# Shifting one weight-conversion step by four slots, starting the last conversion later, and new engine tables, in an attention + SwiGLU kernel

## The chip, the core and the metric

The kernel runs on one core of a Trainium2 chip. The metric is device time in microseconds (us), lower is better. Five engines work side by side, each through its own queue in program order: TensorE (PE: matmuls, and PEld for its weight loads), VectorE (DVE), ScalarE (ACT), GpSimd (POOL) and SyncE (SP), which here only issues DMAs. Semaphores tie them together: an instruction waits until those that it depends on are done, and everything behind it on its own queue waits too.

## What is computed

All arrays are float32.

```
q, k, v: (8 batches, 8 heads, 576 tokens, 64);  tau = 0.02
scores = q k^T / 8
scores = where(scores >= rowmax(scores) - tau, scores, -1e9)
attn   = exp(scores - rowmax) / (sum + 1e-9)
x      = (attn v), heads side by side                # 4608 x 512
g      = x @ w_gate;  val = x @ w_val                # 512 -> 1536
out    = (g * sigmoid(g) * val) @ w_out              # 1536 -> 512
```

Weights arrive as 64-bit floats. The kernel turns each one into a 32-bit float itself, from the two 32-bit words of every number.

## The kernel before

**Two phases.** The first batch is treated apart from the other seven. It runs as 20 *first-batch slots*, one for each tile of 128 queries (64 in a last tile) of a pair of heads. Segments `n` = 0 to 3 hold two tiles each, segments 4 to 7 three; `x` counts tiles in a segment. The fifth slot is (n, x) = (2, 0), the ninth (4, 0), the tenth (4, 1). The other batches run as *main slots* s = 0, 1, 2, ..., twelve to a batch, three to a pair of heads.

**A first-batch slot** (function body after `last = iter(())`): PE computes scores (`sc`, L438, or L444 for a 64-row tile) into one of two PSUM buffers per tile half; DVE takes the negated row maxima (`nm`, L455); ACT computes thresholds and exponentials (L458, L459); DVE masks them and sums them (L462), then L464 and L465 give the reciprocal `ri`; from the ninth slot on one half of the tile is scaled by ACT (L472) and the other by POOL (L470). In the next slot PE transposes the tile (`tp`, L506; L508 in the first eight slots) and ACT copies it out (L515, L519, L522); in the slot after, PE multiplies with v (`xa`, L539, L541). From the ninth slot, PE fills in matmuls of the gate and value products (`pg`, `pv`, L555).

**Weight steps.** There are 24 pieces of 128 x 768 elements, numbered here from 0 in the order of their fetches: 16 of w_gate and w_val, 8 of w_out. Each takes:

1. *fetch* (`fetch_weights`, L282 as a pair of DMAs or L279 as one, on SP). It is issued only when the landing place is free;
2. *split* (`split_weights`, ACT, L298 and L299), the sign-free high part and the low part;
3. *clamp* (POOL, L291; `clamp_split`);
4. *shift* (`shift_weights`, DVE, L318);
5. *join* (`join_weights`, DVE, L324), in the next slot just after L455; it frees the landing place;
6. *add* (`add_lower`, POOL, L334): one directly after the joins of the slot, one more behind the scaling L470 and the clamp L291 of the same slot, if pieces wait.

In steady state slot k splits piece k-2, shifts piece k-3 and joins piece k-4. A last tile of a segment in segments 4 to 6 is a *double* slot: it shifts two pieces behind its matmuls, and the slot after joins two. `shift_weights` and `fetch_weights` in a slot move whatever is next in line, so that holding one step back moves all later pieces back by a slot until a slot takes two.

Between these come other steps: SP issues the loads of q, k and v (L367, L417, L418), 8 at a time in flight by its semaphores; POOL scales the queries (L371, with the whole `qT` of segment 8 in the tenth slot); DVE transposes them (L669, L754).

**The main slots** are written by a planner (class `Plan`). Each instruction is a job with an engine, an estimated duration, dependencies and a rank; whenever an engine is free in the plan, the ready job of the best rank and earliest time is emitted next. So the order of each queue follows from estimated times, and a small edit reorders much. In a main slot DVE takes maxima (`mx`, L1726, L1728); a copy across partitions is done by DVE (L1734, L1735) or, for slots in `FIRST_MAX_BY_ACT`, by ACT (L1740, then L1744 on DVE); then come thresholds (L1747), six exponentials (L1751), six masks (L1753), an exchange of sums (L1761), `ri` (L1766, L1767), six scalings by ACT (L1779) or, for as many as `FIRST_POOLED` says, by POOL (L1776), and three transposes (L1781). The scores of slot s+1 (L1705) need the masks of slot s, because they reuse its PSUM.

The two tables hold for main slots 0 to 23 (batches 1 and 2). `rest_of_weights` plans what is left of the weights at main slot 0: the last pieces 21 to 23, with ACT jobs L873 and L876, a clamp on DVE (L291) for the last two, L883 and L885 on DVE (shift and join) and L887 on POOL (add). Only piece 23 is still to be fetched then (L864). Weight pieces that were fetched earlier count as landed at plan time 6.3; the one still to be fetched is ready for L873 when its planned DMA ends.

Of the kernel before, what the change touches and what calls it, by code (L numbers as in the profile page):

```python
# [27 lines left out]
class Plan:  # L28
# [12 lines left out]
    def job(self, eng, took, fn, *deps, rank=1, lag=0.0, moves=0.0):  # L41
        j = Job(eng, took, fn, rank, lag, moves)
        for d in deps:
            if isinstance(d, Job) and d.end is None:
                d.then.append(j)
                j.waits += 1
            elif d is not None:
                j.ready = max(j.ready, self.after(d, eng) if isinstance(d, Job) else d + self.HOP)
        if not j.waits:
            self.open[eng].append(j)  # L50
        return j
# [61 lines left out]
def kernel(  # L113
# [14 lines left out]
    NP = H // 2  # L128
# [106 lines left out]
    def give_back(ps):  # L235
        turns.append(taken.pop(id(ps))[0])

    def run_idle(n):
        ps = bank("idle")
        for _ in range(n):  # L240
            nc.tensor.matmul(ps[:, 0:TC], ones[:, 0:P], ones, start=True, stop=True)
        give_back(ps)
# [62 lines left out]
    def clamp_split():  # L305
        while unclamped:
            dst = unclamped.popleft()
            clamp(nc.gpsimd, dst)
            clamped.append(dst)

    def shift_weights(n=1):

        steps = [split.popleft() for _ in range(min(n, len(split)))]
        if any(up is x for up, place, lo in steps for x in unclamped):
            clamp_split()
        for up, place, lo in steps:
            ub = up.bitcast(U32)
            nc.vector.tensor_scalar(out=ub, in0=ub, scalar1=3, scalar2=None, op0=ALU.logical_shift_left)  # L318
        shifted.extend(steps)

    def join_weights():
        for up, place, lo in shifted:
            ub = up.bitcast(U32)
            nc.vector.scalar_tensor_tensor(out=ub, in0=words(place, up, 1), scalar=0x80000000, in1=ub,  # L324
                                           op0=ALU.bitwise_and, op1=ALU.bitwise_xor)
            used.discard(place)
        unsummed.extend(shifted)
        shifted.clear()
        add_lower(min(1, len(unsummed)))
# [348 lines left out]
    def give(unit):  # L678
        ready.append(unit)
        left[0] += cost(unit)  # L680
# [19 lines left out]
    for n, seg in enumerate(segs[:2 * NP]):  # L700
        early_slots[0] = n < NP
        if n >= NP:
            seg["v"] = segs[seg["i"]]["v"]
        for x, t in enumerate(seg["tiles"]):
            go = scores(seg, t)
            next(go)
            join_weights()
            if not n and not x:
                run_idle(6)
            next(last, None)  # L710
            box = []
            if n < NP:
                attend_tile(lambda *y: box.extend(y))
            else:
                attend_tile()
            flips = flip_steps()
            if n >= NP and x == 1:
                next(flips, None)
            next(go)
            if box:  # L720
                box[1]()
                give_back(box[0])
            next(last, None)
            for _ in flips:
                pass
            if n == NP and x == 0:
                attend_tile()
                give(FIRST)
            part = pace(n, x) / 2
            more = len(split)  # L730
            if n or x:
                split_weights()
                fetch_weights(2)
            next(go)
            clamp_split()
            add_lower(1)
            double = t == NT and NP <= n < NP + 3
            if more and not double:
                shift_weights()
            fill(part)  # L740
            next(go)
            fill(part)
            if double:
                shift_weights(2)
                split_weights()
                clamp_split()
                fetch_weights(2)
            gates()
            last = go
            if n == NP - 1 and x == 0:  # L750
                later.rotate(1)
            if later and (n == NP or n == NP - 1 and x == 0):
                to, fr = later.popleft()
                nc.vector.transpose(out=to, in_=fr)  # L754
            if x == 0 and 0 < n < NP - 1:
                load_v(segs[n + 1])
                more_loads.popleft()()
            if n == 0 and x == 1 or n == 1:
                scales.popleft()()
            elif n == NP - 2 and x == 1:  # L760
                more_loads.popleft()()
                scales.popleft()()
            elif n == NP - 1:
                scales.popleft()()
                fetch_qk(NP)
            elif n == NP and x == 1:
                scales.popleft()()
            if x == len(seg["tiles"]) - 2 and n + 1 < len(segs):
                prepare(segs[n + 1])
# [8 lines left out]
    job, pe = plan.job, plan.pe  # L778
# [72 lines left out]
    def rest_of_weights():  # L851

        todo = [(dst, None, place, lo) for dst, place, lo in split] + [(dst, None, place, None) for dst, place in fetched]
        landed = 6.3
        todo += [(dst, srcs, place, None) for dst, srcs, place in wpieces]
        done, joins = {}, []
        for n, (dst, srcs, place, lo) in enumerate(todo):
            m = dst.shape[1]
            j = None
            under = done.get((NW // 3 - len(todo) + n) // 2)  # L860
            if srcs:
                def fetch(dst=dst, srcs=srcs, place=place):
                    to = places[place].bitcast(U64).rearrange("p (m n) -> p m n", m=nf)
                    nc.sync.dma_start(out=to, in_=srcs[0])  # L864

                j = job("SP", 0.1, fetch, done.get(place), lag=5.0)
            if lo is None:
                lo = los[0].rearrange("p (m n) -> p m n", m=m)
                los.rotate(1)
                before = joins[-3] if len(joins) > 2 else None  # L870

                def up_part(dst=dst, place=place):
                    nc.scalar.activation(dst, words(place, dst, 1).bitcast(F32), AF.Abs, scale=2.0 ** -96)  # L873

                def lo_part(dst=dst, place=place, lo=lo):
                    nc.scalar.activation(lo, words(place, dst, 0), AF.Identity, bias=minus2, scale=-2.0 ** -51)  # L876

                j = job("ACT", 0.93, up_part, j if srcs else landed, done.get(place), under, rank=2)
                j = job("ACT", 1.03, lo_part, j, before, rank=2)
            ub = dst.bitcast(U32)  # L880
            if not any(dst is x for x in clamped):
                j = job("DVE", 0.6, lambda dst=dst: clamp(nc.vector, dst), j, rank=2)
            j = job("DVE", 0.6, lambda ub=ub: nc.vector.tensor_scalar(  # L883
                out=ub, in0=ub, scalar1=3, scalar2=None, op0=ALU.logical_shift_left), j, rank=2)
            j = job("DVE", 0.96, lambda ub=ub, dst=dst, place=place: nc.vector.scalar_tensor_tensor(  # L885
                out=ub, in0=words(place, dst, 1), scalar=0x80000000, in1=ub, op0=ALU.bitwise_and, op1=ALU.bitwise_xor), j, rank=2)
            j = job("POOL", 1.85, lambda ub=ub, lo=lo: nc.gpsimd.tensor_tensor(out=ub, in0=ub, in1=lo.bitcast(U32), op=ALU.add), j, rank=2)  # L887
            joins.append(j)
            done[place] = j
        return joins  # L890
# [1013 lines left out]
    CH = {0: 2, 1: 3, 10: 4, 11: 4}  # L1904
    POOLED = {1: 3, 3: 2, 6: 3, 7: 2, 11: 1}
    MAX_BY_ACT = (0, 3, 5, 6, 8, 9, 10)
    FIRST_POOLED = {0: 2, 1: 2, 4: 1, 6: 1, 7: 2, 8: 2, 10: 1, 11: 1, 12: 2, 13: 2, 14: 3, 15: 3, 17: 2, 18: 1, 19: 3, 20: 1, 21: 1, 22: 1, 23: 3}
    FIRST_MAX_BY_ACT = (0, 1, 2, 3, 6, 9, 12, 15, 16, 18, 20, 21)
    CD = {0: 1, 1: 1, 9: 2, 10: 2, 11: 2}
    PLAIN = {0: 2, 1: 2, 2: 3, 3: 1, 4: 2, 5: 3, 6: 1, 7: 2}  # L1910
    CH0 = {8: 3, 9: 2, 10: 4, 11: 3, 12: 2}
# [42 lines left out]
    for s, (n, x) in enumerate((n, x) for n in range(len(halved)) for x in range(NU3)):  # L1954
# [13 lines left out]
        elif s == 1:  # L1968
            box = []
            m = pe(1.0, lambda: attend_tile(lambda *y: box.extend(y)))  # L1970
            j = job("ACT", 0.27, box[1], m, rank=0)
# [4 lines left out]
        if s == 1:  # L1976
            prepare_v(seg)
        at_, pooled, max_by_act = (kk, POOLED, MAX_BY_ACT) if b > DEEP else (s, FIRST_POOLED, FIRST_MAX_BY_ACT)
        slot_rest(seg, t, pss, mark, pooled.get(at_, 0), at_ in max_by_act, 1 if x == NU3 - 1 else 2)
        if x == 0 and n + 1 < len(halved):  # L1980
            prepare_next(i + 1, plan.t)
        if s == 0:
            joins = rest_of_weights()
# [3 lines left out]
        if s in WS:  # L1987
            g, place = WS[s]
# [24 lines left out]
    for c in (B - 1, B):  # L2013
# [4 lines left out]
        if c < B:  # L2018
            w = SM // 2
            j = []  # L2020
# [43 lines left out]
```

## Time and profile before

| what | value |
|---|---|
| median of 3 runs | 1373.76 us (1372.51 to 1375.14) |
| profiled execution | 1371.38 us, of which the program's span is 1369.2 us |
| PE busy in the span | 1351.0 us, 99% |
| DVE, ACT, POOL busy | 78%, 64%, 53% |
| PE idle from 0 to 160 us of the span, summed over 10 us stretches | 11.4 us |
| PE idle from 160 to 420 us | 1.4 us |
| granted TensorE clock, all 10 us stretches to 420 us | 1.00 |
| first-batch slots end, main slot 0 begins (first L1705) | 130.69 us |

The profile is of one execution, and all steps are worked out against its own times; what lies around its span is 1371.38 - 1369.2 = 2.2 us. Its views are: a page of totals; the chain of waits that ended last (at each step what released it); the list of who waited for whom; and a timeline of instructions with their start, duration, engine, line and, in brackets, the idle time of the engine before it and what ended it. Matmul ends are modelled, so an idle PE is counted only where the next matmul starts late.

### The profile page before, as it was taken

To read this page: it belongs to the slowest core of one execution; us is meant where nothing else is said; L and a number is where in the kernel's file an instruction comes from. 1 tells how busy PE (TensorE), PEld (TensorE's weight loads), DVE (VectorE), ACT (ScalarE), POOL (GpSimd) and SP (SyncE) were. 2 spreads that over 40 slices of the span, in tenths; PEclk is the share of its full clock that TensorE was granted. 3 is DMA by queue.
4 is the path that set the end of the run, shared out by engine and by line. 5 is a ranking of instruction groups with operands and counts; after the bars stand their busy time and mean duration, and the time that the engine had idled before them with its cause. 6 is when DMAs were issued, how large, how long until landed. Compare 5 with 4: busy or idle time off the path is not lost.

```text
span 1369.2 us, 39187 instructions
## 1 busy us (share of the span) xinstructions
PE 1351.0 (99%) x15590; PEld 1116.1 (82%) x15590; DVE 1070.9 (78%) x2815; ACT 875.5 (64%) x2277; POOL 719.9 (53%) x665
## 2 busy tenths in 40 slices
PE   8999999999999999999999999999999999999998
PEld 7777787778788788877887888877887788999998
DVE  7878888887887777777778777777777776787786
ACT  6888776666756766677776766776767764330330
POOL 2688598663564669434973387427943593000000
PEclk9999999999999999999999999999999999999999
DMA  8752424545525540654154513553165403524411
GB/s 177 200 185 90 82 60 133 146 121 156 151 52 155 144 98 27 181 159 117 37 171 128 150 36 128 144 144 87 36 192 144 113 19 143 162 78 146 151 66 32
DMA packets 208294, 162.32 MB, mean 119 GB/s; under 512 B 166128, under 2 KB 180464, under 8 KB 202736
## 3 DMA queue, kind: packets, MB, share of 16 engines
q1 hardware_dynamic: 203920, 158.86, 41.3%
q8 instruction: 124, 2.03, 0.6%
q10 hardware_dynamic: 4192, 0.95, 0.3%
q14 instruction: 58, 0.48, 0.1%
HBM read 138.28 MB, written 21.50 MB: 117 GB/s over the span
## 4 chain that ended last, share of the span: by engine, by line
PE 90%; DVE 3%; DMA 2%; POOL 2%; SPq 1%; issue 1%; ACT 1%; ACTq 0%; DVEq 0%; POOLq 0%
PE pb L993 18%; PE pa L993 12%; PE px L1473 12%; PE sc L1705 10%; PE pe L993 9%; PE xa L1802 9%; PE po L1269 5%; PE py L1482 5%; PE sc L1154 2%; PE pg L1200 2%; PE pv L1200 2%; PE pe L1154 1%; SPq L367 1%; DMA wo<-in_moe_w_val_dram 1%; PE sc L1473 1%
## 5 line engine op out<-in xcount | busy, mean ns | idle before, releaser
L1753 DVE SCALAR_TENSOR_TENSOR pall<-sc,th,pall 128x288 f32<-128x288 f32 x504 | 244.0, 514 | 65.1 <-ACT pall L1751 50.7
L993 PE MATMUL pb<-xall,big 128*128 128x256 f32 x1152 | 273.5, 380 | 0.0
L1751 ACT ACTIVATE pall<-sc,nm 128x288 f32<-128x288 f32 x504 | 232.2, 498 | 34.1 <-DVE pall L1753 33.8
L993 PEld LDWEIGHTS pb<-xall,big 128*128 128x128 f32 x1152 | 216.4, 190 | 31.0 <-issue 2.2
L1781 DVE STREAM_TRANSPOSE pall<-pall 128x576 f32<-128x576 f32 x252 | 189.7, 765 | 58.2 <-ACT pall L1779 41.4
L1779 ACT ACTIVATE pall<-pall,ri 128x288 f32<-128x288 f32 x415 | 189.8, 529 | 26.3 <-DVE ri L1767 25.8
L846 POOL TENSOR_TENSOR hall<-hall,tmp 128x512 f32<-128x512 f32 x80 | 102.3, 1279 | 159.3 <-DVE hall L1046 141.9
L993 PE MATMUL pa<-xall,big 128*128 128x256 f32 x768 | 183.4, 382 | 0.0
L993 PEld LDWEIGHTS pa<-xall,big 128*128 128x128 f32 x768 | 143.0, 190 | 22.2 <-issue 2.7
L1705 PE MATMUL sc<-kT,qT 64*32 64x144 f32 (+1 forms) x5376 | 150.0, 345 | 2.9 <-DVE pall L1753 1.7
L1726 DVE TENSOR_REDUCE mx<-sc 128x2 f32<-128x576 f32 x168 | 124.8, 743 | 28.6 <-PE sc L1705 28.1
L1705 PEld LDWEIGHTS sc<-kT,qT 64*32 64x32 f32 x5376 | 97.8, 106 | 56.9 <-issue 21.0
L993 PE MATMUL pe<-xall,big 128*128 128x256 f32 x576 | 137.2, 381 | 0.4 <-issue 0.4
L1802 PE MATMUL xa<-pall,vall 64*32 64x288 f32 x4032 | 133.0, 404 | 0.9 <-DVE hall L1046 0.8
L1776 POOL TENSOR_SCALAR pall<-pall,ri 128x288 f32<-128x288 f32 x89 | 88.9, 1010 | 67.0 <-DVE ri L1767 63.8
L993 PEld LDWEIGHTS pe<-xall,big 128*128 128x128 f32 x576 | 108.5, 190 | 17.3 <-issue 2.8
L1802 PEld LDWEIGHTS xa<-pall,vall 64*32 64x32 f32 x4032 | 76.5, 107 | 50.6 <-issue 7.4
L1761 ACT COPY sums<-sums 32x6 f32<-32x6 f32 x336 | 66.8, 199 | 45.6 <-DVE pall L1753 41.1
L1045 ACT ACTIVATE vall<-tmp 128x512 f32<-128x512 f32 x96 | 60.2, 630 | 24.6 <-DVE tmp L1058 9.0
L1482 PE MATMUL py<-wo,hall 128*128 128x256 f32 x336 | 74.8, 379 | 0.0
L1728 DVE TENSOR_REDUCE mx<-sc 128x1 f32<-128x288 f32 x168 | 74.8, 445 | 0.0
L846 POOL TENSOR_TENSOR tmp<-tmp 128x512 f32<-128x512 f32 x36 | 45.9, 1276 | 53.4 <-ACT tmp L1068 53.4
(258 smaller groups left out, 2481.3 us busy)
## 6 DMA issues: line engine op xcount, KB each, us to landing
big<-sums_hbm SPq DMA_DIRECT2D x42, 1024.0 KB, 5.4
big<-sums_hbm SPq DMA_DIRECT2D x48, 768.0 KB, 4.7
vall<-in_v_dram SPq DMA_DIRECT2D x112, 144.0 KB, 3.0
out_dram<-big SPq DMA_DIRECT2D x32, 256.0 KB, 3.0
qT<-in_q_dram SPq DMA_DIRECT2D x112, 72.0 KB, 4.8
kT<-in_k_dram SPq DMA_DIRECT2D x112, 72.0 KB, 3.0
wo<-in_moe_w_gate_dram SPq DMA_DIRECT2D x16, 384.0 KB, 4.1
wo<-in_moe_w_val_dram SPq DMA_DIRECT2D x16, 384.0 KB, 4.8
```

Of the source, the lines that this page charges most:

```text
L846: return lambda: nc.gpsimd.tensor_tensor(out=out, in0=a, in1=b, op=op)
L993: nc.tensor.matmul(ps[:, i], w[:, k_, i * P:(i + 1) * P], x[:, k_, :], start=first and i == k_ == 0, stop=True, skip_group_check=True)
L1473: nc.tensor.matmul(ps, a[:, f, :], ws[n][:, f, :], start=bank_ not in begun, stop=True, skip_group_check=True)
L1482: nc.tensor.matmul(ps(), a[:, f, i * P:(i + 1) * P], operands[o][:, f, :], start=first and f == 0, stop=True, skip_group_check=True)
L1705: nc.tensor.matmul(pss[h][(slice(g * G, (g + 1) * G), *part)], qT[hs, col:col + G], kT[hs, c * SH + keys[0]:c * SH + keys[1]], start=True, ...
L1726: rs.append(job("DVE", 0.72, lambda n=n, tile_=tile_: nc.vector.tensor_reduce(out=mx[:, n:n + 2, 0], in_=tile_[:, :, 0:SH], axis=AX.X, op= ...
L1751: ej = job("ACT", 0.42, lambda x=x, n=n: nc.scalar.activation(ps[x], scs[x], AF.Exp, bias=nm[:, n:n + 1]), ej, *((masks[h, 0], masks[h, 1] ...
L1753: masks[x] = job("DVE", 0.45, lambda x=x, n=n: nc.vector.scalar_tensor_tensor(out=ps[x], in0=scs[x], scalar=th[:, n:n + 1], in1=ps[x], op0 ...
L1776: scaled.append(job("POOL", 1.02, lambda x=x, n=n: nc.gpsimd.tensor_scalar(out=x, in0=x, scalar1=ri[:, n:n + 1], scalar2=None, op0=ALU.mul ...
L1779: scaled.append(job("ACT", 0.46, lambda x=x, n=n: nc.scalar.activation(x, x, AF.Copy, scale=ri[:, n:n + 1]), rj, rank=rank))
L1781: seg["turned"].append(job("DVE", 0.72, lambda both=both: nc.vector.transpose(out=both, in_=both), *scaled, rank=rank))
L1802: nc.tensor.matmul(holds[a].ap()[x * G:(x + 1) * G, 0:SH].rearrange("d (i q) -> d i q", q=G), vr[rs, h, j, ds], p[rs, h, :, j, :], start=( ...
```

## The change

Three edits:

- **The step in the fifth slot is left out** (`(n, x) != (NP - 2, 0)`, with NP = 4), and **the ninth slot shifts two pieces** (`1 + (n == NP and x == 0)`). Pieces 2 to 5 are thus shifted and joined one slot later each; in the ninth slot pieces 5 and 6 are shifted, in the tenth both are joined; from piece 7 on everything is in its old slot.
- **A weight that is still to be fetched at main slot 0 (piece 23) is not ready for L873 before plan time 19.0**; it had been ready when its DMA was planned to end.
- **Both tables have new entries.** The number of scalings on POOL changes in main slots 3, 6, 8, 12 to 17 and 21 to 23; ACT takes over the exchange of maxima in slots 10, 17 and 23, and gives up that of slot 16.

```
-            if more and not double:
-                shift_weights()
+            if more and not double and (n, x) != (NP - 2, 0):
+                shift_weights(1 + (n == NP and x == 0))
...
-        landed = 6.3
+        landed, begins = 6.3, 19.0
...
-                j = job("ACT", 0.93, up_part, j if srcs else landed, done.get(place), under, rank=2)
+                j = job("ACT", 0.93, up_part, *((j, begins) if srcs else (landed,)), done.get(place), under, rank=2)
...
-    FIRST_POOLED = {0: 2, 1: 2, 4: 1, 6: 1, 7: 2, 8: 2, 10: 1, 11: 1, 12: 2, 13: 2, 14: 3, 15: 3, 17: 2, 18: 1, 19: 3, 20: 1, 21: 1, 22: 1, 23: 3}
-    FIRST_MAX_BY_ACT = (0, 1, 2, 3, 6, 9, 12, 15, 16, 18, 20, 21)
+    FIRST_POOLED = {0: 2, 1: 2, 3: 1, 4: 1, 6: 3, 7: 2, 8: 1, 10: 1, 11: 1, 12: 3, 13: 1, 15: 2, 16: 3, 17: 3, 18: 1, 19: 3, 20: 1, 22: 2, 23: 2}
+    FIRST_MAX_BY_ACT = (0, 1, 2, 3, 6, 9, 10, 12, 15, 17, 18, 20, 21, 23)
```

How the queues stand after the change, by the programs alone (no times): PE's order is the same. On SP the fetch of piece 6 goes from ahead of the second group of four query loads (`extra<-in_q_dram`, L367) to behind it, and that of piece 7 from ahead of the eight loads of `qT` and `kT` to behind them. On DVE one L318 and one L324 go from the fifth and sixth slot to the ninth (two L318) and the tenth (two L324 between L455 and L462). On POOL the tenth slot's order becomes L334, L470, L291, L334, L371, where it had been L334, L470, L291, L371. ACT's order is the same until main slot 1; there L873 of piece 23 goes from ahead of L1740 to behind the exponentials and L1209, ahead of L1761. On DVE, L885 of piece 23 goes to main slot 3, between the maxima and L1744. From main slot 4 on, the jobs of DVE, ACT and POOL are reordered in places down to slot 23.

## The prediction

> **What bounds the kernel now.** I read the page's totals first, then who waited for whom on PE, then the chain of waits around the slots that the diff touches, then the timeline of single instructions.
>
> ```profile
> PE 1351.0 (99%) x15590; PEld 1116.1 (82%) x15590; DVE 1070.9 (78%) x2815; ACT 875.5 (64%) x2277; POOL 719.9 (53%) x665
> ```
>
> PE is busy 99% of 1369.2 us, and the diff leaves its instructions and their order alone. The time can move only by the places where PE stands still: it can win no more than the waits now there, and it loses whatever new wait it causes. PE's waits from 57 to 157 us (total, how often, longest):
>
> ```profile
> PE sc L438 <- DVE pall L462: 2.2, 3, 0.9
> PE tp L506 <- POOL pall L470: 1.4, 3, 0.5
> PE sc L1705 <- DVE pall L1753: 1.2, 1, 1.2
> PE pg L1200 <- ACT big L522: 0.6, 1, 0.6
> ```
>
> So in the first batch PE's scores wait for DVE's masks. The chain of waits says why (start, duration, what; parts of it from 57 to 92 us):
>
> ```profile
> 62.80 0.87 DVE big L324
> 63.66 1.58 DVE pall L462 x4
> ...
> 67.64 1.05 POOL big L291
> 68.69 1.70 POOL qT L371
> 70.39 1.80 POOL big L334
> 72.19 1.11 POOL big L291
> 73.33 0.04 DVE big L318
> ...
> 75.62 1.94 DVE big L324 x2
> 77.56 1.49 DVE pall L462 x4
> ```
>
> From the tenth slot on, the end is set by DVE's join and masks, then by POOL without a gap, then by DVE again, up to the scores at 78.44. Work added to this row of steps is added to the time.
>
> **Edit 1, what is taken out of the fifth and sixth slots.** Away go one shift (L318 at 33.07, 0.88 us) and one join (L324 at 36.20, 1.46 us) ahead of the masks at 37.58, for which PE waited:
>
> ```profile
> 38.54 1.94 PE L438 MATMUL sc<-pall,qT 64*128 64x288 f32 x8 [1.09 <-DVE pall L462]
> 40.05 0.91 ACT L298 ACTIVATE big<-wo 128x768 f32<-128x768 f32 x1 [1.37 <-DMA wo<-in_moe_w_val_dram]
> 42.21 1.05 PE L508 MATMUL tp<-pall 128*128 128x128 f32 x7 [0.28 <-ACT pall L478]
> ```
>
> The 1.09 us at the scores would go. But PE's next step but one, the transposes at 42.21, already waits 0.28 us for ACT's L478, and that stands in ACT's queue behind the split L298, which waited 1.37 us for a weight DMA (issued 34.24, landed 39.97). The edit brings that DMA no earlier, so ACT still ends L478 at about 42.2 and PE starts the transposes at 42.21. The wait at the scores becomes a wait at the transposes: **gain 0** (at most the 1.09, if that DMA came earlier too).
>
> **Edit 1, SP's queue.** Joins that come a slot later free landing places later. Piece 6's pair of DMAs, issued at 43.19 and 43.59, goes behind four query loads, to about 45.0; by the trace's median of 4.9 to 5.5 us for such a pair it lands near 50, and its split ran at 50.42: about 0.3 us to spare. Piece 7's pair, issued at 46.12 and 46.55, goes behind eight loads of qT and kT, which were issued from 47.49 to 54.93. It is then issued between some 51 and 55.6, landing between 56 and 59.95 (the pair issued at 55.04 and 55.64 landed then). Its split stands at 57.78 in ACT's queue, ahead of L472, which releases PE's transposes at 61.40 with 1.1 us to spare. I take 0, the value of the earlier issue; the later one delays L472 by 2.2 us and PE by 1.1. Range 0 to +1.2.
>
> **Edit 1, the step given back.** The ninth slot's second shift lies in DVE's idle 4.19 us ahead of L455 at 61.38: 0. In the tenth slot a second join comes between L455 and the masks:
>
> ```profile
> 62.72 0.95 DVE L324 SCALAR_TENSOR_TENSOR big<-wo,big 128x768 uint32<-128x768 uint32 x1
> 65.79 1.88 POOL L470 TENSOR_SCALAR pall<-pall,ri 128x576 f32<-128x576 f32 x1 [0.22 <-DVE ri L465]
> 70.36 1.83 POOL L334 TENSOR_TENSOR big<-big 128x768 uint32<-128x768 uint32 x1
> 78.44 1.82 PE L438 MATMUL sc<-pall 64*128 64x288 f32 x9 [0.82 <-DVE pall L462]
> ```
>
> One more join is 0.95 us; the masks, `ri` at 65.45 and POOL's L470 at 65.79 come that much later. Behind the new wait on POOL stand L291, L371, L334 and L291, back to back to 73.29, and DVE's shift waits for the last. Among them comes one more add, L334 of piece 6, between L291 and L371: 1.83 us. (The other L334, ahead of L470, was there already and ends at 65.57, in time.) Both terms lie on the chain that ends at 78.44: 0.95 + 1.82 = **+2.77**; PE's wait there becomes some 2.7 to 3.6 us. From below: +1.8, if the join were hidden but the add not. From above: 1.46 for the join (its cost at 36.20) and 2.46 for the add (the longest at 76.76), +3.9. I take 2.77, since most neighbours of the same shape take 0.95 and 1.82. I expect no recovery behind it: the next waits of this kind fall at 98.10 and 117.78, a period of 19.66 us, a loop of PE, DVE and POOL in which each waits for the other, and the slots after are unchanged.
>
> A sentence of the Trainium skill speaks against such a wait. The row first: the granted clock is 1.00 in every 10 us stretch to 420 us, with no PE wait over 1.17 us there after the start. The page "TensorE: Matmul & The Clock Gate", section "Why this matters for your kernels", allows no PE gap over about 3 us, and its Part 1 gives half clock after an idle window of about 3.4 us. The new wait of 2.7 to 3.6 us comes close to it; no run here shows one, and by the page a closed gate would add an estimated 1.7 us (half of a 3.4 us window), by the row nothing. The sum leaves it out.
>
> **Edit 2, the last split begins later.** In main slot 1 ACT held up the exchange of maxima for a weight DMA, issued 140.08 and landed 146.52:
>
> ```profile
> 146.54 0.93 ACT L873 ACTIVATE wo<-extra 128x768 f32<-128x768 f32 x1 [0.41 <-DMA extra<-in_moe_w_out_dram]
> 147.49 0.81 ACT L1740 COPY mx<-mx 32x6 f32<-32x6 f32 x4
> 153.06 1.32 PE L1705 MATMUL sc<-kT,qT 64*32 64x288 f32 x19 [1.17 <-DVE pall L1753]
> ```
>
> With L873 gone from there, L1740 starts near 146.6, 0.9 earlier, and the exponentials lose L876 ahead of them too: from 149.43 to about 147.95. The masks, which ended at 153.34, end about 1.4 earlier, near 151.95, and PE, free at 151.89, starts without the 1.17 us. These scores also ran stretched by the masks (one per 1.84 us where others take 1.43): 0.41 more. Less 0.2 for a new small wait: 1.17 + 0.41 - 0.2 = **-1.35** (0 to -1.58). What is late next: the join L885 of piece 23 moves to main slot 3, between the maxima and L1744 (at 171.23). It costs 0.94 to 1.38 us by the other joins, and that slot's masks (end 175.31) have only 0.19 us ahead of the next scores (175.50): 1.1 - 0.2 = **+0.9** (0.3, if half of it lies in the 0.20 and 0.16 us idle that DVE has there, to 1.2).
>
> **Edit 3, the tables.** From main slot 3 to 23, PE's remaining waits at the scores are 0.41 (at 184.78), 0.41 (215.94), 1.2 (279.5), 0.5 (291.3) and 0.64 (344.35): 3.2 us. In slot 4 the transpose L1846 (0.78 at 183.44) goes from between the masks to ahead of them, which I value at -0.35 of the 0.41; in slot 13 a scaling less on POOL gives -0.3, in slot 14 one more on DVE's side +0.25; the other changed slots have 1.3 to 3.5 us between masks and next scores, which cover a transfer of one scaling (0.53 on ACT). I take **-0.35**; ends -3.2 (all waits gone) and +1.0 (new ones in slots 12 to 17).
>
> **Sum.** 2.77 - 1.35 + 0.9 - 0.35 = +1.97. Against the profiled execution's own 1371.38 (span 1369.2 and 2.2 around it) that is 1373.35. The median of the three runs is 1373.76, 2.4 above the profiled one, so the predicted median is 1373.76 + 1.97 = **1375.7**.
>
> **Rivals.**
> - *Slower, plainly:* piece 7's weights land late on ACT's queue in the ninth slot. For it: eight loads now go ahead of them on SP. Against it: each load is small, and 46 to 55 us has pauses. It decides once they land after about 58.9 (57.78 + 1.1). Price +1.1, beside the add at its contended 2.46 (+0.6): 1375.7 + 1.1 to 1.7, about **1377.2**.
> - *Faster:* ACT's splits and POOL's clamps don't depend on PE and run on while PE waits at 78.44; then the later waits, 0.7 each at 98.10 and 117.78 and three of 0.5 at the transposes, up to 2.8 us, vanish and pay edit 1 back. For it: POOL waited 1.54 us for ACT's L298 at 93.63. Against it: the loop runs through PE. With the forecast's other terms -0.8; with all of the tables' 3.2 us and 0.3 for L885, -4.25. That is 1369.5 to 1373.0, its middle **1371.2**.
> - *The change does nothing that shows:* the add finds room after all, edits 2 and 3 return what 1 takes, within 0.5 of **1373.8**.
>
> **How the numbers follow.** 0.2%, or 2.75 us, is about what a measurement of this kernel can tell from no change. Forecast 0.42, its own range 1374.2 to 1377.3, with 0.27 within 0.2% and 0.15 slower; the late weights 0.25, all slower; the payback 0.25, with 0.15 faster and 0.10 within; no effect 0.08. Faster 0.15, same 0.45, slower 0.40. The range must reach into both other cases: 1371.0 leaves out 0.13 of the payback case, 1378.6 leaves out 0.07 of the others.
>
> **What would show it.** Right: scores of the 12th slot near 81 instead of 78.44 with PE waiting 2.5 us or more; two L324 back to back at 62.7 and POOL without a gap from L470 to the last L291; transposes at 42.2 still waiting, now about 1.4 us; no wait at main slot 1's end, a new one of 0.9 at the scores near 175.5. Wrong: main slot 0 beginning no later than 130.69, L298 near 57.8 waiting for a DMA, waits at 98 and 118 gone, or a granted clock under 1.00.

## The result, and the profile after

Twenty executions of each kernel: the changed one has a median of 1374.72 us (1373.31 to 1377.09), the one before 1372.74 (1369.92 to 1375.14). The ratio is 1.0017, 95% interval 1.0011 to 1.0024. By the medians that is 1.98 us longer, with 1375.7 and +1.97 predicted. The profiled execution took 1374.33 us, its span 1372.5 against 1369.2.

The forecast's sum came out. Not all of its terms did, as the profile after shows. The page's totals:

```profile
PE 1353.8 (99%) x15590; PEld 1116.7 (81%) x15590; DVE 1068.8 (78%) x2807; ACT 875.1 (64%) x2284; POOL 719.8 (52%) x666
```

The same 15590 matmuls keep PE busy 2.8 us longer than before. So a part of the loss is no wait at all: the matmuls ran slower. Who waited for whom on PE from 57 to 157 us (total, times, longest):

```profile
PE sc L438 <- DVE pall L462: 4.8, 3, 3.2
PE tp L506 <- POOL pall L470: 0.9, 2, 0.5
PE pg L1200 <- ACT big L522: 0.6, 1, 0.6
PE sc L444 <- DVE pall L462: 0.6, 1, 0.6
```

The wait of 1.2 us at the main slots' scores (L1705) is gone; one wait of 3.2 us at the first batch's scores is new. The chain of waits up to it:

```profile
63.15 1.73 DVE big L324 x2
...
68.77 1.05 POOL big L291
69.82 1.78 POOL big L334
71.60 1.70 POOL qT L371
73.30 2.09 POOL big L334
75.39 0.81 POOL big L291
76.23 0.04 DVE big L318
...
79.13 1.73 DVE big L324 x2
80.86 0.75 DVE pall L462 x2
```

This is the forecast's chain with the second join at its head (63.15) and the second add in its middle (69.82). PE's timeline at the two places that edit 1 touches:

```profile
37.46 1.72 PE L438 MATMUL sc<-pall,qT 64*128 64x288 f32 x8
42.62 2.05 PE L508 MATMUL tp<-pall 128*128 128x128 f32 x16 [2.00 <-ACT pall L478]
65.67 1.19 PE L444 MATMUL sc<-pall 64*64 64x288 f32 x8 [0.56 <-DVE pall L462]
81.74 3.21 PE L438 MATMUL sc<-pall 64*128 64x288 f32 x10 [3.23 <-DVE pall L462]
```

The wait at the seventh slot's scores is gone (37.46, no bracket) and stands at the transposes instead, 2.00 us. The scores at 81.74 come 3.30 us later than before, and they took 3.21 us where the same ten took 2.06. The view by stretches shows why; the columns are the stretch, busy time of PE, PEld, DVE, ACT and POOL, then the granted clock, the DMA share and GB/s:

```profile
78.00:80.00 2.00, 0.51 (x3) 0.11 (x1) 2.00 (x4) 1.50 (x4) 0.52 (x1) 1.00 0.00 0
80.00:82.00 2.00, 0.26 (x1) 0.29 (x2) 2.00 (x4) 1.63 (x4) 1.93 (x1) 0.97 0.46 65
82.00:84.00 2.00, 2.00 (x9) 1.78 (x9) 1.20 (x6) 1.44 (x2) 1.63 (x2) 0.50 1.03 402
84.00:86.00 2.00, 2.00 (x19) 1.12 (x18) 1.68 (x3) 0.23 (x1) 2.00 (x3) 0.50 0.81 324
86.00:88.00 2.00, 2.00 (x10) 2.00 (x11) 2.00 (x1) 0.65 (x2) 1.34 (x1) 0.50 0.00 0
88.00:90.00 2.00, 2.00 (x10) 1.80 (x9) 1.15 (x4) 2.00 (x6) 1.77 (x1) 0.82 0.43 57
```

PE stands still from 78.5 to 81.7, and the granted clock then falls to 0.50 for 6.8 us. Below this is called half clock, or the clock gate closing. How far the changed kernel lies behind the one before, by the start of PE's scores, is the ledger of the whole change:

| scores that start in the changed kernel at | behind by | what happened since the line above |
|---|---|---|
| 60.46 (tenth slot) | 0.36 | transposes at 42.62 |
| 72.22 (twelfth) | 0.89 | second join |
| 81.74 (thirteenth) | 3.30 | second add on POOL, a slower shift, shorter joins |
| 90.77 (fourteenth) | 6.21 | half clock |
| 136.16 (main slot 0) | 5.47 | a later wait at the transposes that vanished |
| 157.29 (main slot 2) | 4.23 | edit 2 |
| 179.50 (main slot 4) | 4.00 | edit 2, with L885 |
| 406.20 (main slot 24) | 3.50 | edit 3 |

### The profile page after: what moved, and what is told of

The parts are those of the page before. It is cut to its first block, busy times and chain, and to the rows that moved or that the text cites. A ratio compares the mean times of both kernels' runs of the same rounds, so it can differ in the third digit from the quotient of the medians.

```text
span 1372.5 us, 39182 instructions
## 1 busy us (share of the span) xinstructions
PE 1353.8 (99%) x15590; PEld 1116.7 (81%) x15590; DVE 1068.8 (78%) x2807; ACT 875.1 (64%) x2284; POOL 719.8 (52%) x666
## 4 chain that ended last, share of the span: by engine, by line
PE 92%; DVE 2%; POOL 2%; DMA 1%; SPq 1%; issue 1%; ACT 0%; ACTq 0%; DVEq 0%; POOLq 0%
PE pb L993 18%; PE pa L993 12%; PE px L1473 12%; PE sc L1705 10%; PE pe L993 9%; PE xa L1802 9%; PE po L1269 5%; PE py L1482 5%; PE pg L1200 2%; PE pv L1200 2%; PE sc L1154 2%; PE pe L1154 1%; SPq L367 1%; PE sc L1473 1%; PE sc L438 1%
## 5 line engine op out<-in xcount | busy, mean ns | idle before, releaser
L1705 PE MATMUL sc<-kT,qT 64*32 64x144 f32 (+1 forms) x5376 | 149.3, 345 | 1.7 <-issue 1.0
L1705 PEld LDWEIGHTS sc<-kT,qT 64*32 64x32 f32 x5376 | 97.4, 106 | 55.9 <-issue 19.1
L1761 ACT COPY sums<-sums 32x6 f32<-32x6 f32 x336 | 66.5, 198 | 45.4 <-DVE pall L1753 40.8
L1740 ACT COPY mx<-mx 32x6 f32<-32x6 f32 x196 | 38.1, 194 | 59.6 <-DVE mx L1728 57.7
```

The lines of the kernel that those rows point to most:

```text
L1705: nc.tensor.matmul(pss[h][(slice(g * G, (g + 1) * G), *part)], qT[hs, col:col + G], kT[hs, c * SH + keys[0]:c * SH + keys[1]], start=True, ...
```

## The experiments

Each kernel ran with the kernel before on the same chip, the ratios being to that. What the executions' mean granted clock says turned out to be the key, so the table has it. One window of half clock is 3.41 us (shown below) and lowers the mean by about 0.001; an execution at 1.000 is called open.

| kernel | median us | before, same chip | ratio, 95% interval | executions at clock 1.000 / 0.999 / less | median at 1.000 |
|---|---|---|---|---|---|
| edit 1 alone | 1375.80 | 1370.89 | 1.0034 (1.0020 to 1.0048) | 0 / 0 / 6 | - |
| edit 2 alone | 1369.67 | 1370.89 | 0.9994 (0.9983 to 1.0005) | 6 / 2 / 4 | 1368.74 |
| edits 2 and 3 | 1369.28 | 1370.89 | 0.9988 (0.9978 to 0.9999) | 5 / 2 / 5 | 1368.24 |
| changed, PE kept busy in its wait | 1372.74 | 1370.89 | 1.0008 (0.9997 to 1.0018) | 5 / 4 / 2 | 1370.99 |
| before, 6 memsets | 1376.45 | 1371.37 | 1.0035 (1.0024 to 1.0047) | 0 / 0 / 12 | - |
| before, 14 memsets | 1378.87 | 1371.37 | 1.0053 (1.0038 to 1.0067) | 0 / 0 / 6 | - |
| changed, one add later | 1374.30 | 1371.37 | 1.0016 (1.0008 to 1.0024) | 0 / 3 / 9 | - |
| before, PE kept busy at the seventh slot | 1370.66 | 1371.37 | 0.9992 (0.9983 to 1.0002) | 7 / 4 / 1 | 1370.65 |
| edits 2 and 3, PE kept busy there | 1370.03 | 1372.91 | 0.9978 (0.9969 to 0.9987) | 8 / 0 / 2 | 1369.90 |
| the same, one transpose earlier | 1369.60 | 1372.91 | 0.9978 (0.9968 to 0.9988) | 7 / 0 / 1 | 1369.52 |
| before, 3 memsets | 1376.81 | 1372.91 | 1.0020 (1.0010 to 1.0031) | 0 / 3 / 9 | - |
| edit 3 alone | 1374.73 | 1372.91 | 1.0009 (0.9998 to 1.0021) | 3 / 0 / 8 | 1371.62 |
| the kernel before, with rows 1 to 4 | 1370.89 | | | 12 / 5 / 13 | 1369.83 |
| the kernel before, with rows 5 to 8 | 1371.37 | | | 11 / 6 / 12 | 1370.50 |
| the kernel before, with rows 9 to 12 | 1372.91 | | | 10 / 3 / 18 | 1370.92 |

All 20 executions of the changed kernel had a mean clock of 0.996 to 0.998. Of the 90 of the kernel before in the last three rows, 33 had 1.000. Where a kernel's executions fall into groups by the clock, its median moves with their shares, so that the difference of two medians and the ratio can be about 1 us apart (the changed kernel with one add later, and 3 memsets).

**1. Edit 1 alone.**

```
+            if more and not double and (n, x) != (NP - 2, 0):
+                shift_weights(1 + (n == NP and x == 0))
```

> The kernel before with edit 1 alone. Theory A (the wait closes the clock gate): PE waits about 3.2 us for the masks near 78.5, the granted clock falls to 0.50 for some 6 to 7 us behind it, and main slot 0 begins about 5.5 us later than the kernel before (136.2 instead of 130.7); the time is 4.5 to 5.5 us longer. Theory B (the forecast's +2.77 is right and the half clock of the changed kernel was a chance of one execution or comes from edits 2 and 3): granted clock 1.00, time 2.5 to 3 us longer.

It took 4.9 us more than the kernel before, PE waited 3.2 us at the thirteenth slot's scores, the clock was low in all six executions, and main slot 0 began at 135.70. Theory A: edit 1 carries the loss, and the half clock belongs to it.

**2. Edit 2 alone.**

```
+        landed, begins = 6.3, 19.0
+                j = job("ACT", 0.93, up_part, *((j, begins) if srcs else (landed,)), done.get(place), under, rank=2)
```

> The kernel before with edit 2 alone (the old tables). Theory A: the wait of 1.17 us at the end of main slot 1 goes and L885 finds room, so the scores of main slot 4 come 1.2 to 1.4 us earlier and the time is 1 to 1.5 us shorter. Theory B (the forecast): L885 gives 0.9 us back at main slot 3, and the time is 0.45 us shorter.

The median is 1.2 us shorter, that of the executions at clock 1.000 1.1 us (1368.74 against 1369.83); the interval reaches past 1. In the traces, the way from main slot 0's scores to main slot 23's is 258.30 us against 259.80. So -1.1 to -1.5, theory A. The profiled execution brought something that nobody had asked for. Its scores of the seventh slot, and the clock behind them (columns as above):

```profile
39.37 2.65 PE L438 MATMUL sc<-pall,qT 64*128 64x288 f32 x8 [1.98 <-DVE pall L462]
```

```profile
38.00:40.00 2.00, 0.63 (x3) 0.55 (x4) 1.97 (x6) 1.52 (x5) 1.43 (x1) 1.00 1.00 359
40.00:42.00 2.00, 2.00 (x9) 1.04 (x7) 1.44 (x4) 1.67 (x2) 1.04 (x2) 0.62 1.04 363
42.00:44.00 2.00, 2.00 (x18) 1.67 (x17) 1.94 (x3) 2.00 (x7) 1.45 (x3) 0.50 0.97 170
44.00:46.00 2.00, 2.00 (x10) 2.00 (x11) 1.93 (x8) 0.59 (x2) 1.59 (x1) 0.50 0.90 250
46.00:48.00 2.00, 2.00 (x14) 1.76 (x13) 0.46 (x2) 0.74 (x2) 0.00 (x0) 0.68 1.15 255
```

This stretch is untouched by edit 2: it is the kernel before. There the wait was 1.09 us in the profile that I predicted from; here it is 1.98, and half clock followed it. POOL's timeline, of before and then of this run, shows where the 0.9 us come from:

```profile
28.75 0.93 POOL L371 TENSOR_SCALAR hall<-hall,scl 128x256 f32<-128x256 f32 x1 [4.57 <-DMA hall<-in_q_dram]
```

```profile
29.82 1.48 POOL L371 TENSOR_SCALAR hall<-hall,scl 128x256 f32<-128x256 f32 x1 [5.68 <-DMA hall<-in_q_dram]
```

A load of queries landed about a us later, and behind L371 stand an add, a clamp, DVE's shift, its join and the masks. So the kernel before has a half clock of its own, in executions in which this load is late. The other profiles with the same first seven slots bear this out: in runs 2, 3, 5, 11 and 12 this L371 begins at 29.48 us or later and the wait is 1.85 to 1.99 us, and in all of them but run 3 the clock fell; in run 6 it begins at 29.13, the wait is 1.09 as in the profile of before, and the clock stayed.

**3. Edits 2 and 3 together,** the first batch as before.

> The kernel before with edits 2 and 3, the first batch as it was. Theory A: what the changed kernel's trace shows behind main slot 0 comes alone: 1.3 us from edit 2 and 0.5 to 0.7 from the tables, so 1.8 to 2.1 us shorter, and faster than both kernels. Theory B (the forecast): -1.35 + 0.9 - 0.35, 0.8 us shorter.

1.6 us shorter, at clock 1.000 too (1368.24 against 1369.83); main slot 0 to 23 takes 257.96 us. Theory A within 0.2.

**4. The changed kernel with PE kept busy in its wait.**

```
+            if (n, x) == (NP + 1, 1):
+                run_idle(6); turns.appendleft(turns.pop())
             go = scores(seg, t)
```

> The changed kernel with six matmuls of ones (128x256, into a free PSUM bank, read by nobody) ahead of the scores for which PE waits 3.23 us; they need nothing but the bank, so they run in the wait and leave some 1.8 us of it. Theory A (idleness closes the gate): granted clock 1.00 throughout, and the 2.9 us lost between 81.7 and 90.8 come back: 2.5 to 3 us shorter than the changed kernel, about 1 us shorter than the kernel before. Theory B (the lower clock has another cause, and the wait itself is the price): the same clock and the same time as the changed kernel, or longer by up to 0.3.

```profile
77.05 2.75 PE L241 MATMUL idle<-pall 128*128 128x256 f32 x12
80.35 2.09 PE L438 MATMUL sc<-pall 64*128 64x288 f32 x10 [0.55 <-DVE pall L462]
```

```profile
80.00:90.00 10.00, 9.44 (x77) 7.09 (x77) 8.56 (x19) 8.25 (x16) 9.64 (x6) 1.00 0.69 235
```

Six matmuls are twelve passes; their bank goes back to the front, so that the later steps keep theirs. The wait is filled to 0.55 us and the clock stays at 1.00 here (second view, columns as above). In five of eleven executions the mean is 1.000, where the changed kernel has none. Theory A for the place. Against the kernel before it is 1.9 us longer by the medians (the interval reaches past 1), not 1 shorter, so the size I expected was wrong; part of the other six executions' loss probably lies elsewhere (run 7 shows a place). Row 4 against row 3 of the table, both at clock 1.000, is edit 1 without a half clock: 1370.99 - 1368.24 = **2.75 us**, from five executions each. The two traces agree: from the tenth slot's scores to the thirteenth's it is 21.19 us in run 4 and 18.30 in run 3, 2.89 less.

**5 and 6. The kernel before with PE made to wait,** no weight step moved.

```
             join_weights()
+            for _ in range(6 if (n, x) == (NP + 1, 0) else 0):     # then 14
+                nc.vector.memset(ones, 1.0)
```

> The kernel before with six memsets of a constant (128x256, the values it already has) on DVE ahead of the masks of the 12th slot: PE's wait for them, 0.82 us before, becomes some 2.1 us (0.2 to 0.27 us a memset). Theory A (a wait of PE closes the clock gate; one of 1.98 us did it in the run of edit 2 alone, one of 1.94 us in the run of edits 2 and 3 did not): the gate closes here in some executions and not in others; where it stays open the time is 1.3 us longer than the kernel before, where it closes 4 to 4.5. Theory B (only the long wait of over 3 us closes it): granted clock no lower than that of the kernel before, 1.3 us longer.

> The same with fourteen memsets: PE waits some 3.6 us, with no step of the weights moved. Theory A (the wait itself closes the gate): granted clock 0.50 for 6 to 7 us behind the wait in every execution, 2.8 us for the wait and 2.2 to 2.9 for the clock, 5 to 5.7 us longer than the kernel before. Theory B (the gate closed because of what edit 1 moves, not because PE stood still): clock as in the kernel before, 2.8 us longer.

```profile
82.07 3.21 PE L438 MATMUL sc<-pall 64*128 64x288 f32 x10 [2.96 <-DVE pall L462]
```

```profile
82.00:83.00 1.00, 0.93 (x3) 0.82 (x5) 0.93 (x5) 0.00 (x0) 0.00 (x0) 0.50 1.01 406
```

```profile
84.00 3.21 PE L438 MATMUL sc<-pall 64*128 64x288 f32 x10 [6.09 <-DVE pall L462]
```

The first two views are of six memsets, the third of fourteen. A memset costs 0.37 us, not 0.2 to 0.27, so the waits are 2.96 and 6.09 us. Every execution of both has a low clock; in the profiled ones half clock begins at 81.8 us, 0.3 ahead of the end of the wait, and at 80.7, in the middle of it. Theory A: the waiting does it and not what edit 1 moves. Theory B of run 5 falls too: under 3 us suffices. Against the open executions of the kernel before (1370.50) they lose 5.95 and 8.37 us, of which 2.1 and 5.3 are the longer wait; the rest, 3.8 and 3.1, is the clock, here and in some executions at the seventh slot.

**7. The changed kernel, with the second add left to the next slot.**

```
-            add_lower(1)
+            add_lower(int((n, x) != (NP, 1)))
```

> The changed kernel with the tenth slot's second add left to the next slot, where it runs behind the clamp that DVE waits for. Theory A: PE's wait of 3.23 us falls by the add's 1.8 us to about 1.4, the gate stays open, and the time is 4 to 4.5 us shorter than the changed kernel: 1 to 1.5 us shorter than the kernel before. Theory B (the add only moves the wait: ACT's split waits for the place that the add frees, or the chain is held elsewhere): less than 1 us of the wait goes and the gate closes still.

```profile
43.46 3.03 PE L508 MATMUL tp<-pall 128*128 128x128 f32 x16 [2.75 <-ACT pall L478]
```

```profile
76.28 2.17 DVE L318 TENSOR_SCALAR big<-big 128x768 uint32<-128x768 uint32 x1 [0.72 <-POOL big L291]
```

Missed: 2.9 us longer than the kernel before by the medians, 2.2 by the ratio. The wait at the scores fell only from 3.23 to 2.29 us. DVE's shift begins sooner, but beside the add it takes 2.17 us (1.17 in the changed kernel, 0.56 in the one before), and that eats 1.0 of the 1.8. And the first line is the place left over from run 4: the wait that edit 1 moved to the transposes was 2.75 us in this execution, and half clock followed it at 44.3.

**8. The kernel before with PE kept busy at the seventh slot,** as in run 4 but four matmuls at `(NP - 1, 0)`.

> The kernel before with four matmuls of ones (128x256, nobody reads them) ahead of the scores of the seventh slot, for which PE waits 1.1 to 2.0 us (38.54 in the profile of before). Theory A (in some executions of the kernel before that wait closes the gate for 7 us, and this is what spreads its times over 6 us): granted clock 1.00 in all or nearly all executions, times within 2 us of each other, median that of the open executions of the kernel before, 1 to 1.5 us under its median. Theory B (the low clocks of the kernel before come from elsewhere): the same spread and the same clocks.

Eleven of twelve executions at 0.999 or more, where the kernel before has 17 of 29; the median is 0.7 us shorter, less than the 1 to 1.5 expected, and the interval reaches past 1. Theory A for the clocks. Not for the times: they still spread over 4.3 us (1369.51 to 1373.84). The filler itself takes 1.99 us, which is longer than the wait of 1.09 us that there is where the load is early.

**9 and 10. The best version that the runs point to:** edits 2 and 3 with that filler; then also the transpose L754 ahead of the eleventh slot's shifts.

> Edits 2 and 3 with the first batch as it was, and the four matmuls of ones ahead of the seventh slot's scores. Theory A (edit 1 costs, edits 2 and 3 gain 1.6 us with the gate open, the matmuls of ones keep the gate open): granted clock 0.999 to 1.000 in nearly all executions, 2 to 3 us shorter than the median of the kernel before, faster than both kernels. Theory B (the two gains overlap): no better than edits 2 and 3 alone, 1.6 us shorter.

> The same with one transpose of the eleventh slot (0.51 us, L754) ahead of its two shifts instead of behind them: in the profile of before DVE stands idle 0.72 us ahead of the second shift, waiting for POOL's clamp, and the transpose could run there. Theory A (the chain through POOL's clamp, the shift, the maxima, the joins and the masks sets PE's wait at 78.44): that wait falls by about 0.5 us and the time with it, 0.5 us under the run without it. Theory B (the wait is set elsewhere): no change.

Both have a ratio of 0.9978 to the kernel before, 2.9 and 3.3 us shorter by the medians: a little faster than the kernel before, and so than the changed one, which is slower than that. Moving the transpose did nothing to the wait (0.79 us after 0.82): theory B. The shift moved up, and the joins behind it took 2.40 us for two instead of 2.00.

**11. Three memsets.**

> The kernel before with three memsets instead of six ahead of the masks of the 12th slot. By the runs with six (wait 2.96 us) and fourteen (6.09) a memset costs 0.37 us, so PE waits some 1.9 us. Theory A (waits near 2 us close the gate in a part of the executions only): +1.1 us where the gate stays open, 2 to 3 us more where it closes; granted clocks between those of the kernel before and of the run with six. Theory B (a wait under 2 us never closes it): clocks as in the kernel before, 1.1 us longer.

```profile
82.70 2.06 PE L438 MATMUL sc<-pall 64*128 64x288 f32 x10 [1.79 <-DVE pall L462]
```

```profile
85.00:86.00 1.00, 1.00 (x17) 0.88 (x14) 1.00 (x2) 0.00 (x0) 1.00 (x2) 0.50 0.69 276
```

The profile shows 1.79 us of wait at the scores, and half clock behind it, from 84.7 us on. No execution has 1.000, where ten of 31 of the kernel before have it, and nine of twelve are at 0.996 or less. Theory A: waits under 2 us close the gate often. By the medians the time is 3.9 us longer (2.7 by the ratio), for 1 us of added wait; but in the profiled execution only one of three windows of half clock is this wait's, and two are the seventh slot's, as in run 2.

**12. Edit 3 alone.**

> The kernel before with edit 3 alone (the new tables, the old time at which the last split may begin). Theory A (the tables' gain of 0.3 to 0.5 us, the difference between edits 2 and 3 and edit 2, is their own): 0.3 to 0.5 us shorter than the kernel before, the wait of 1.17 us at the end of main slot 1 unchanged. Theory B (the new entries fit only a plan in which edit 2 stands): no gain or up to 1 us longer.

1.8 us longer by the medians, mostly because eight of its eleven executions had a low clock; at 1.000 it is 0.7 us longer (three executions, 2.1 us apart), and main slot 0 to 23 takes 260.26 us against 259.80 in one trace, in which the wait at the end of main slot 1 is 1.46 us. So 0.5 to 0.7 longer, as far as these few can tell: theory B, the new entries pay only in the plan that edit 2 makes.

## Why the prediction was right, and where it was not

**The fifth and sixth slot, gain 0.** Right in kind: the wait moved to the transposes (2.00 us, about 1.4 forecast, since ACT's weight DMA landed at 40.39 and not 39.97). But it was worked out from one execution. The wait that edit 1 takes out is 1.09 us in some executions and 1.85 to 1.99 in others, and in four of five profiles of the latter half clock followed; edit 1 moves that wait as well, and run 7 shows half clock behind it at the transposes.

**SP's queue.** Right that it costs nothing. ACT waited 0.48 us for piece 7's weights, until 58.72, and had still 1.31 us idle after L472 (60.43). The rival decided from 58.9; it came within 0.2 us. This wait of L298, and the granted clock under 1.00, are two of the four signs that I had named for being wrong; the first cost PE nothing, the second cost 2.9 us.

**The step given back, +2.77.** Right: 3.30 - 0.36 = 2.94 in the trace, 2.75 by the medians of runs 3 and 4. The second join cost 0.87 (0.95 forecast), the add 1.78 (1.82), and 0.61 is a shift that took longer, 1.17 us instead of 0.56; against these 3.26 us stand 0.3 from shorter steps, above all the two joins at 79.13 (1.73 us where they had taken 1.94). I named the scores at 78.44 as the twelfth slot's; they are the thirteenth's.

**"The sum leaves it out": the clock, the step that failed.** The granted clock fell, at a cost of 2.9 us (3.30 to 6.21 behind), about as much as the step given back. The wait was 3.23 us, inside the 2.7 to 3.6 that I had named for it. The trace had no wait over 1.17 us after the start that could show it, so the row gave no price, and "by the row nothing" was no bound. The Trainium skill, "TensorE: Matmul & The Clock Gate", section "Why this matters for your kernels", warned of it, but its limit of about 3 us is too wide for this case: half clock followed waits of 2.29, 1.98 and 1.79 us too. By Part 1 I estimated one window and 1.7 us; it was two.

**No recovery.** Nearly: of 6.21 us, 0.74 came back by main slot 0. By the fifteenth slot's scores it was 0.87, where the waits at the transposes near 87 and 88 (0.50 us the second) were gone; 0.16 went again at the sixteenth's, which waited 0.63 us instead of 0.47. The payback rival's mechanism worked, at a quarter of its price.

**Edit 2: -1.35 right, +0.9 for L885 wrong.** The trace gives -1.25 by main slot 2. Then no loss at main slot 3 but a further 0.14 to 0.23. DVE's timeline, of before and then of the changed kernel:

```profile
165.59 1.38 DVE L885 SCALAR_TENSOR_TENSOR wo<-extra,wo 128x768 uint32<-128x768 uint32 x1
```

```profile
169.27 0.98 DVE L883 TENSOR_SCALAR wo<-wo 128x768 uint32<-128x768 uint32 x1
...
174.36 1.42 DVE L885 SCALAR_TENSOR_TENSOR wo<-extra,wo 128x768 uint32<-128x768 uint32 x1
```

L885 does stand between the maxima and L1744 now. But it had stood just ahead of the same slot's maxima, and there only the shorter L883 took its place: I counted where the step arrives and not what it leaves. The maxima began 2.57 us after the scores before, 1.78 now.

**Edit 3: -0.35.** Right as a sum (-0.50 in the trace, -0.50 by runs 2 and 3 at clock 1.000), wrong by place: main slot 4 gave nothing, slot 13 took 0.36 and slot 14 gave 0.76, with -0.35, -0.3 and +0.25 forecast. The last two are one place: before, the scores of slot 14 began at 279.51 and stopped for 0.56 us at 280.71; now they wait 0.47 us once, ahead of 283.92. The 3.2 us that I took for the most the tables could win were not there either: PE stood idle for 1.4 us from 160 to 420 us.

**Why the total still fits.** Trace against trace the change is +3.3 us, since the profile of before was an execution without a half clock. By the medians it is +1.98, because the kernel before loses about 3 us to its own half clock in nearly half of its executions (43 of the 90 beside the experiments at 0.998 or less), and its median holds that; the clocks of the result's own twenty are not on record. So the clock's 2.9 us that the sum left out was balanced by the 0.9 for L885 that did not come, by the recovery and by the half clock that the kernel before already had. The number was right partly by luck, by terms that cancelled. Runs 1 and 3 add up to the traces' figure, +4.9 - 1.6 = +3.3 us, against a kernel before with a median of 1370.89 us there and 1372.74 in the result. What is shown is that edit 1 loses (run 1) and edits 2 and 3 together win a little (run 3).

What stays open is why a wait of 1.98 us closes the gate (run 2) and one of 1.94 us in run 3 and of 2.00 us in the changed kernel (at 42.62) did not; in run 9 the clock fell at 120.7, behind a wait of 0.90 us.

## What to carry to other kernels

On a kernel that keeps PE 99% busy, price a new PE wait of about 2 us or more with the clock behind it: the added wait was 2.4 us here, the clock 2.9. Look at the mean clock of every execution before you take the waits of one profile for the kernel's own: a load that lands a us late made another kernel of it. And when a step moves, subtract it where it was before you add it where it goes.

## What the runs showed of the hardware

**Half clock comes in whole windows.** Summed over 1 us stretches, the time at 0.50 was 3.42 and 3.42 us (run 7), 3.40 (run 9), 3.40 and 6.82 (runs 5 and 11, each), 6.82 (runs 1 and 2 and the changed kernel), 6.84 (run 12) and 10.24 (run 6): one, two or three times 3.41. The Trainium skill, "TensorE: Matmul & The Clock Gate", Part 1, states a free-running window of 3413 ns; the runs agree on its length, and on its running free. In the three traces in which the clock fell twice, the two falls, timed in stretches of 0.1 us, are 40.96 us apart (runs 5 and 7) and 44.37 (run 11), 12, 12 and 13 windows of 3413 ns, whatever the waits ahead of them: the falls keep to a grid that no wait starts anew. So a fall can come late: 2.35 us behind the end of the wait at 82.93 in run 7. Whether a wait counts or not by where it lies on this grid is not shown. The idle time in one window doesn't decide it alone: by this grid, 1.71 us of the window that ends at 44.33 in the changed kernel were idle and the clock stayed, and 0.90 us of the one that ends at 120.74 in run 9, and it fell.

**DVE's shift stands still beside POOL's add.** In run 7 the shift, 0.54 us elsewhere in this run (at 68.50 and 83.83), began at 76.28 and took 2.17, while the add ran on POOL from 76.21 to 78.03: it ended 0.42 us after the add. In the changed kernel the shift of 1.17 us stood beside the clamp that ended at 76.98, and it ended 0.42 us after that too:

```profile
76.23 1.17 DVE L318 TENSOR_SCALAR big<-big 128x768 uint32<-128x768 uint32 x1 [2.51 <-POOL big L291]
```

The Trainium skill, "SBUF — State Buffer", section "SBUF: two separate sides", tells of a port pair that the two engines lock for a whole instruction; these two rows agree.
